# The first batch's attention laid out anew: x in runs of 1 KB, scores with tokens in partitions

## The chip, the core and the metric

The kernel runs on one core of a Trainium2 chip. The core has five engines with queues of their own: TensorE (PE, matmuls; PEld is its weight loads), VectorE (DVE), ScalarE (ACT), GpSimd (POOL) and SyncE (SP, which here issues most DMAs). The metric is the device time of one execution in microseconds; lower is better. All data in the compute part are fp32.

## The reference

`x` is (B, H, S, D) = (8, 8, 512, 64), `state` is (8, 8, 32, 64), `w_in` is 512 x 2048 and `w_out` 2048 x 512; the weights arrive as 64-bit floats.

```python
scores  = scale * np.matmul(x, state.transpose(0, 1, 3, 2))      # tokens by states
a       = softmax(scores);   xread = np.matmul(a, state)
scores2 = scale * np.matmul(state, x.transpose(0, 1, 3, 2))      # states by tokens
a2      = softmax(scores2);  sread = np.matmul(a2, x)
y = concat([xread, sread], axis=2)            # (B, H, 512 + 32, D)
y = y.transpose(0, 2, 1, 3).reshape(B * 544, 512)
h = y @ w_in
g = h * erf(softplus(h))
out = g @ w_out                               # (4352, 512)
```

## The kernel before

**Attention folded into the weights.** The kernel never forms `xread`. For each batch and each group of 512 hidden columns it multiplies the states with `w_in` (the "mixed" states, `mixed_part` and `mixed_pair`, tile `m`: 256 rows, one for each head and state) and then multiplies these with the transposed softmax weights `aT` (256 rows by 512 tokens). That product is `h` transposed, in four blocks of 128 hidden columns by 512 tokens. Softplus and erf run on ACT, the product with `h` on DVE, and the second projection accumulates in four PSUM banks `o0` to `o3`.

**Weights.** They come in 16 pieces of 1 MB in the order two of `w_in`, two of `w_out`, and so on (`pieces`, four groups). A piece goes from DRAM into one of three `raw` buffers (`weight`, DMA at L146), and is turned into fp32 by two ACT instructions (L152, L154) and three DVE instructions (L155, L156, L157). After the last of these, `fetch()` issues the DMA of the next piece. `weights_in(j)` gives 256 columns of `w_in` in 2 KB runs of the source; the fp32 copy has the form (partition, piece, k, 256 columns).

**Batch 0.** While the weights arrive, batch 0 alone is worked on, group by group, with products of 512 columns (`first0`, L828: four blocks a group, two matmuls each; `soft` L832; `erf` L835; `times` L839; `project` L626). Later batches (L559, L701) use seven products for eight and keep their operands in other forms. The change touches their part, from about 110 us on, only in the layout of `w_in`.

**The opening, `attention0`.** x of batch 0 comes in four DMAs of 128 tokens each, two from ACT's queue and two from SP's (L111); each run is 64 floats, 256 bytes. The states of batch 0 follow on SP (L114), then the weights. TensorE warms up on the identity (`warm(8)`), transposes x to `xT` (16 transposes, L312, in the order in which the quarters land), transposes the states (`states`, L190, copied by ACT at L191) and makes the scores with states in partitions (`scored`, L205: eight matmuls of 512 tokens on 64x32 tiles). Since the softmax over states needs a state axis within a partition, DVE turns the scores in 32x32 blocks (L225), takes the largest (L227), subtracts (L229); ACT takes the exponential (L230); DVE sums (L236), inverts (L240, L241), multiplies (L243) and turns the result back into `aT` (L329). ACT copies the scores to `sc` (L323) for the second softmax, which follows much later (`rest()`, L332 to L341). Between these stand, at three places, the conversion of the first weight pieces, half of the first mixed states (L455, copied at L457 and L458) and 32 + 5 matmuls on the identity (`after_scores`, `before_sums`, `amid_sums`).

**Order.** The order of instructions on TensorE, DVE, ACT and SP is that of the program text (`in_order`). Queues are worked strictly in turn, so an instruction that waits holds up all behind it on its engine. The states of batches 1 to 7 are loaded by `load_st()` (L120, eight DMAs, 256-byte runs), called at L902, and transposed at L936 in the third group.

Of the kernel before, what the change touches and what calls it, by code (L numbers as in the profile page):

```python
# [9 lines left out]
F32 = mybir.dt.float32  # L10
# [7 lines left out]
def kernel(  # L18
# [90 lines left out]
    x_t[0] = xin.tile([P, NC, H, D], F32, name="x")  # L109
    for c in range(NC):  # L110
        (nc.scalar, nc.sync)[c % 2].dma_start(  # L111
            out=x_t[0][:, c], in_=x[0, :, P * c:P * c + P].rearrange("h p d -> p h d"))
    for e in range(2):
        nc.sync.dma_start(out=st[:, 0, D * e:D * e + D],  # L114
                          in_=state[0].rearrange("(i e) n d -> e i n d", e=2)[e])

    def load_st():
# [6 lines left out]
    w_in = const.tile([P, NF // 4, NK, 2 * P], F32, name="w_in")  # L124
    away = ring[:, :, 2].rearrange("p u k i t -> p u (k i t)").rearrange(
        "p u (j k f) -> p u j k f", k=NK, f=2 * P)
    pieces_in = [w_in[:, j] for j in range(NF // 4)] + \
        [away[:, j // 2, j % 2] for j in range(NF // 4)]
    of_group = [w_in[:, 2 * g:2 * g + 2] for g in range(2)] + [away[:, u] for u in range(2)]
    kept_in = dram.tile([2, P, NF // 4, NK * 2 * P], F32, name="kept_in")  # L130
# [4 lines left out]
    def weight(dst, src, shape):  # L135

        if src.dtype == F32:
            fetched.append(nc.sync.dma_start(out=dst, in_=src))
            return [lambda: None] * 2, [lambda: None] * 3
        i = shape[1]
        raw = act.tile([P, 2 * shape[0] * i], U32, name="raw", bufs=3)
        fetched.append(nc.sync.dma_start(out=raw.rearrange("p (o i) -> p o i", i=2 * i),  # L146
                                         in_=src.bitcast(U32)))
        words = raw.rearrange("p (n w) -> p n w", w=2)
        lo, hi = words[:, :, 0], words[:, :, 1]
        dst = dst.rearrange("p o i -> p (o i)")  # L150
        d = dst.bitcast(U32)
        return [lambda: nc.scalar.activation(out=dst, in_=hi.bitcast(F32), func=ACTF.Copy,  # L152
                                             scale=2.0 ** -112),
                lambda: nc.scalar.activation(out=lo, in_=lo, func=ACTF.Copy, scale=2.0 ** -29)], \  # L154
            [lambda: nc.vector.tensor_scalar(d, d, 3, None, op0=ALU.logical_shift_left),  # L155
             lambda: nc.vector.tensor_tensor(d, d, lo, op=ALU.add),  # L156
             lambda: nc.vector.scalar_tensor_tensor(out=d, in0=hi, scalar=0x80000000, in1=d,  # L157
                                                    op0=ALU.bitwise_and, op1=ALU.bitwise_or)]
# [3 lines left out]
    def weights_in(j):  # L162
        return weight(pieces_in[j],
                      moe_w_in[:, 2 * P * j:2 * P * j + 2 * P].rearrange("(k p) f -> p k f", p=P),
                      (NK, 2 * P))

    def weights_out(j):
        return weight(w_out[:, 2 * j:2 * j + 2, :],
                      moe_w_out[2 * P * j:2 * P * j + 2 * P].rearrange("(t p) e -> p t e", p=P),
                      (2, d_model))  # L170

    spare = ps_o.tile([P, d_model], F32, name="o3")
# [9 lines left out]
    sT = const.tile([P, NK, B, Ns], F32, name="sT")  # L182
    aT = {}

    def states(bs, pool=ps_at, name="at"):


        ps = pool.tile([P, len(bs), P], F32, name=name)
        for k, b in enumerate(bs):
            last = nc.tensor.transpose(out=ps[:, k], in_=st[:, b, :], identity=ident)  # L190
        nc.scalar.copy(st[:, bs[0]:bs[-1] + 1, :], ps)  # L191
        return last

    over = lambda t: t.unsqueeze(2).to_broadcast([P, NC * NI, Ns])

# [23 lines left out]
    def states_weights(b, sc, both):  # L219

        aT[b] = keep.tile([P, 2, S], F32, name="aT")
        a = both[:, 0:2].rearrange("p e (k n) -> p e k n", n=Ns)
        m1 = small.tile([P, 2, NC * NI], F32, name="m1")
        for e in range(2):
            nc.vector.transpose(out=both[:, e], in_=sc[e])  # L225
        for e in range(2):
            nc.vector.reduce_max(out=m1[:, e], in_=a[:, e], axis=AX.X)  # L227
        for e in range(2):
            nc.vector.tensor_tensor(a[:, e], a[:, e], over(m1[:, e]), op=ALU.subtract)  # L229
            nc.scalar.activation(out=a[:, e], in_=a[:, e], func=ACTF.Exp, scale=scale)  # L230
        return a

    def sums(a):
        z1 = small.tile([P, 2, NC * NI], F32, name="z1")
        for e in range(2):
            nc.vector.reduce_sum(out=z1[:, e], in_=a[:, e], axis=AX.X)  # L236
        return z1

    def normalise(a, z1):
        nc.vector.tensor_scalar(z1, z1, 1e-9, None, op0=ALU.add)  # L240
        nc.vector.reciprocal(z1, z1)  # L241
        for e in range(2):
            nc.vector.tensor_tensor(a[:, e], a[:, e], over(z1[:, e]), op=ALU.mult)  # L243

# [14 lines left out]

    def inverse(z):  # L260
        nc.vector.tensor_scalar(z, z, 1e-9, None, op0=ALU.add)
        nc.vector.reciprocal(z, z)
# [37 lines left out]
    def attention0(between):  # L300

        xt = x_t[0]
        xT = att.tile([P, NI, S], F32, name="xT")
        xp = [ps_o.tile([P, S], F32, name="o%d" % i) for i in range(3)]
        xp.append(ps_h.tile([P, S], F32, name="h"))
        for c in 1, 0, 2, 3:
            if c == 2:
                warm(3)  # L310
            for i in range(NI):
                nc.tensor.transpose(out=xp[i][:, P * c:P * c + P],  # L312
                                    in_=xt[:, c, 2 * i:2 * i + 2, :], identity=ident)
        for i in range(NI):
            (nc.scalar.copy, nc.vector.tensor_copy)[i % 2](xT[:, i, :], xp[i])
        states(range(1), ps_h, "h")
        s2 = scored(0, xT)
        between[0]()
        both = att.tile([P, NI, S], F32, name="xT")
        sc = att.tile([P, 2, S], F32, name="sc")  # L320
        a = states_weights(0, s2, both)
        for e in range(2):
            nc.scalar.copy(sc[:, e], s2[e])  # L323
        between[1]()
        z1 = sums(a)
        between[2]()
        normalise(a, z1)
        for e in range(2):
            nc.vector.transpose(out=aT[0][:, e], in_=both[:, e])  # L329

        def rest():
            a2 = both[:, 2:4]  # L332
            m2 = largest(sc)
            yield
            z2 = weigh_tokens(sc, m2, a2)
            inverse(z2)
            yield
            a2T = turn_weights(a2)
            yield
            read_tokens(0, a2T, z2)  # L340
            yield  # L341

        return rest()

    def all_of(jobs):
        for f in jobs:
            f()
# [914 lines left out]
```

## Time and profile before

| | |
|---|---|
| median of 8 runs | 725.71 us (725.48 to 726.61) |
| the profiled execution | 725.54 us, its span 723.7 us |
| granted TensorE clock | 1.00 |
| first product with `aT` (L828) | at 22.00 us |
| TensorE busy from 0 to 22 us | 17.95 us, of which the identity matmuls of L177 are most |
| DVE busy from 10 to 20 us | 8.38 of 10 us |
| ACT busy from 25 to 40 us | 14.66 of 15 us |
| TensorE busy from 40 to 100 us | 59.88 of 60 us |

Times within the execution count from the start of the span. The profile lists, for each instruction, its start, its length and what ended the idle time before it; from this it builds a chain that leads from the last instruction back to the first. An engine's instructions overlap a little at their ends, so where an engine is busy without a break the distance between starts is shorter than one instruction's length. A matmul on fp32 appears as two entries, each with its weight load.

### The profile page before, as it was taken

Reading aid. Unit: us, or ns where it says so; the run is one execution under the profiler, and the core shown is the slowest. Engines: PE = TensorE matmul, PEld = TensorE weight load, DVE = VectorE, ACT = ScalarE, POOL = GpSimd, SP = SyncE. Lnnn points to the kernel's source line nnn. Section 1 sums busy time; section 2 is a strip of 40 time slices with the busy share of each in tenths; the row PEclk is TensorE's granted clock in tenths of the full one; section 3 lists DMA queues with packets and bytes.
Section 4 is the critical chain, followed back from the end, with each engine's and each line's share of the span. In section 5 each row is a group of like instructions: output and inputs, shape, how many; then the busy total and the mean of one; then the engine's idle time right before and its main releaser. Section 6 shows DMA issues by size and latency. Waiting matters only on the chain.

```text
span 723.7 us, 10832 instructions
## 1 busy us (share of the span) xinstructions
PE 713.7 (99%) x4232; PEld 564.3 (78%) x4232; DVE 537.3 (74%) x860; ACT 372.1 (51%) x536; POOL 25.2 (3%) x34
## 2 busy tenths in 40 slices
PE   8899999999999999999999999999999999999997
PEld 7444436588878878887888878887888888889996
DVE  4887779899868988788776967698777756665533
ACT  4899794636363624645346536463464534342340
POOL 0000000000100000000000000000000000000000
PEclk9999999999999999999999999999999999999999
DMA  7568886560239154422714270614232231102101
GB/s 236 180 206 250 227 223 240 140 191 29 41 78 232 21 125 61 109 77 70 125 20 154 59 135 13 175 27 133 45 82 103 72 67 19 39 30 30 20 12 29
DMA packets 142907, 74.64 MB, mean 103 GB/s; under 512 B 127112, under 2 KB 127368, under 8 KB 141320
## 3 DMA queue, kind: packets, MB, share of 16 engines
q1 hardware_dynamic: 136552, 65.89, 32.8%
q0 software_dynamic: 4032, 7.34, 7.5%
q10 hardware_dynamic: 2272, 0.72, 0.5%
q8 instruction: 33, 0.54, 0.4%
q14 instruction: 18, 0.15, 0.1%
HBM read 49.81 MB, written 20.45 MB: 97 GB/s over the span
## 4 chain that ended last, share of the span: by engine, by line
PE 93%; ACT 3%; DVE 2%; DMA 1%; issue 0%; ACTq 0%; DVEq 0%
PE o L701 47%; PE h L559 13%; PE at L559 10%; PE o L626 6%; PE h L604 3%; PE o L676 3%; PE h L828 2%; PE h L442 2%; PE at L442 1%; PE at L285 1%; PE at L828 1%; PE at L455 1%; DMA x<-in_x_dram 1%; PE h L205 1%; ACT L835 1%; PE at L205 0%
## 5 line engine op out<-in xcount | busy, mean ns | idle before, releaser
L701 PE MATMUL o<-w_out,ring 128*128 128x256 f32 x896 | 203.0, 379 | 0.0
L701 PEld LDWEIGHTS o<-w_out,ring 128*128 128x128 f32 x896 | 169.8, 190 | 25.0 <-DVE ring L1074 1.0
L701 PE MATMUL o<-raw,ring 128*128 128x256 f32 x672 | 161.4, 381 | 0.0
L701 PEld LDWEIGHTS o<-raw,ring 128*128 128x128 f32 x672 | 126.5, 190 | 25.9 <-ACT m L444 5.0
L552 ACT ACTIVATE ring<-ring 128x512 f32<-128x512 f32 x112 | 70.6, 631 | 59.9 <-DVE ring L542 59.3
L559 PE MATMUL h<-aT,m 128*128 128x256 f32 x336 | 82.0, 380 | 0.0
L1074 DVE TENSOR_TENSOR ring<-ring 128x1024 f32<-128x1024 f32 x60 | 70.6, 1219 | 3.9 <-ACT ring L616 3.9
L559 PEld LDWEIGHTS h<-aT,m 128*128 128x128 f32 x336 | 63.7, 190 | 10.4 <-DVE ring L542 0.7
L542 DVE TENSOR_TENSOR ring<-ring,at 128x512 f32<-128x512 f32 x84 | 57.1, 680 | 16.9 <-PE at L559 15.2
L626 PE MATMUL o<-w_out,ring 128*128 128x512 f32 x128 | 58.5, 597 | 1.4 <-DVE ring L839 1.4
L686 DVE TENSOR_TENSOR ot<-uv,o 128x256 f32<-128x256 f32 (+1 forms) x56 | 30.9, 553 | 30.4 <-PE o L701 28.4
L542 DVE TENSOR_TENSOR ring<-ring,h 128x512 f32<-128x512 f32 x56 | 38.0, 678 | 19.7 <-PE h L559 19.6
L724 ACT COPY ot<-o 128x256 f32<-128x256 f32 x28 | 10.4, 372 | 79.6 <-PE o L701 79.6
L761 POOL DMA_DIRECT2D out_dram<-ot x28 | 24.5, 943 | 659.4 <-DVE ot L686 609.6
L626 PEld LDWEIGHTS o<-w_out,ring 128*128 128x128 f32 x128 | 23.7, 190 | 29.4 <-issue 24.6
L686 DVE TENSOR_TENSOR ot<-ot,o 128x256 f32<-128x256 f32 x56 | 22.2, 416 | 27.8 <-ACT ot L724 27.7
L574 ACT COPY ring<-h 128x512 f32<-128x512 f32 x28 | 16.4, 586 | 47.9 <-PE h L559 47.9
L733 DVE TENSOR_TENSOR ring<-ring 128x512 f32<-128x512 f32 x56 | 38.6, 689 | 1.4
L734 DVE TENSOR_TENSOR ring<-ring 128x512 f32<-128x512 f32 x56 | 36.3, 685 | 0.0
L565 ACT COPY ring<-h 128x512 f32<-128x512 f32 x28 | 16.4, 586 | 28.3 <-PE h L559 28.3
L616 ACT ACTIVATE ring<-ring 128x2048 f32<-128x2048 f32 x16 | 30.4, 1902 | 0.0
L444 ACT COPY m<-h 128x512 f32<-128x512 f32 x11 | 6.4, 586 | 44.4 <-PE h L442 44.3
(181 smaller groups left out, 971.3 us busy)
## 6 DMA issues: line engine op xcount, KB each, us to landing
w_in<-kept_in SPq DMA_DIRECT2D x7, 2048.0 KB, 8.6
raw<-in_moe_w_in_dram SPq DMA_DIRECT2D x8, 1024.0 KB, 5.6
raw<-in_moe_w_out_dram SPq DMA_DIRECT2D x8, 1024.0 KB, 7.1
out_dram<-ot SPq DMA_DIRECT2D x32, 256.0 KB, 2.2
xq<-in_x_dram SPq DMA_DIRECT2D x112, 64.0 KB, 2.4
x<-in_x_dram SPq DMA_DIRECT2D x56, 128.0 KB, 3.1
out_dram<-ot POOLq DMA_DIRECT2D x28, 256.0 KB, 4.6
sc<-xT SPq DMA_DIRECT2D x112, 32.0 KB, 1.9
```

What stands on the lines that cost most here:

```text
L442: nc.tensor.matmul(out=ps[k][e][q, :], lhsT=st[r, b, q], rhs=of_group[g][r, :, i, :], start=True, stop=True)
L542: add = lambda o, x, y: nc.vector.tensor_tensor(o, x, y, op=ALU.add)
L552: nc.scalar.activation(out=s[k], in_=hs[k], func=ACTF.Softplus)
L559: nc.tensor.matmul(out=out[:, i], lhsT=x[:, q:q + P], rhs=y, start=(first and i == 0), stop=(i == 1), skip_group_check=not first)
L616: nc.scalar.activation(out=s, in_=s, func=ACTF.Erf)
L626: nc.tensor.matmul(out=acc[r], lhsT=gT[:, i, P * r:P * r + P], rhs=w_out[:, GF * g + i, :], start=(g == 0 and i == 0), stop=(g == NG - 1 a ...
L686: add = lambda o, x, y: tt(o, x, y, op=ALU.add)
L701: nc.tensor.matmul(out=out, lhsT=lhs[:, i, :], rhs=rhs[:, g, i, :], start=(start and i == 0), stop=(i == GF - 1), skip_group_check=not start)
L733: return [lambda: tt(S1, A21, A22, op=ALU.add), lambda: tt(S2, S1, A11, op=ALU.subtract), lambda: tt(S3, A11, A21, op=ALU.subtract), lambd ...
L734: lambda: tt(S3, A11, A21, op=ALU.subtract), lambda: tt(S4, A12, S2, op=ALU.subtract)]
L761: nc.gpsimd.dma_start(out=rows[2 * h + r][:, c], in_=ot[:, c], accum_op=ALU.add)
L1074: nc.vector.tensor_tensor(s[:, ks], s[:, ks], hs[:, ks], op=ALU.mult)
```

## The change

**x and the states.** x of batch 0 now comes in four DMAs by pairs of heads. Partition p gets tokens 4p to 4p+3, so each run is 4 x 64 floats, 1 KB. The rows of `out` for batch 0 are addressed in the same order (`put_x`). The states of batch 0 come twice side by side, (4 heads x 32 states) in partitions, two groups of heads, in two DMAs on SP between the second and the fourth of x.

**Scores.** For each head, a tile of two tokens-quarters by 64 channels is transposed to `xT` (128 x 128). A block-diagonal tile `bd` holds, for each head, its transposed states twice, so that one matmul of 128 rows gives the scores of two token quarters, with tokens in partitions (`score`: 16 matmuls of 64 columns). The states axis lies within a partition, and the softmax (`less`, `total`, `shared`) runs by two groups of four heads straight from PSUM; its weights are then transposed on TensorE (four transposes a group) and copied by ACT (`keep_a`). The scores with states in partitions, for the second softmax, are 32 matmuls of 128 columns on 64x32 tiles; they stay in the banks `o2` and `o3` until DVE copies them (`keep_scores`). 16 matmuls on the identity follow them, where 32 and 5 stood.

**Weights.** `w_in` is kept as (partition, block of 128 columns, k, 128 columns); each piece is fetched in two DMAs of 128 columns, with runs of 1 KB. The first piece is converted in two halves (two sets of two ACT and three DVE instructions), and the first mixed states of group 0 are made in quarters, quarter, half.

**States of the other batches.** `load_st()` is called before the opening, behind the first three pieces; their transposes go to the first group, in banks `o0` and `o1`, with ACT's copies behind the first erf.

**Other places.** The mixed states of batch 0 are placed by the table `where`, which gives each head its group and its 32 partitions. The identity matmuls write a bank of the pool `ps_h` in place of `o3`. `hidden_states`, `combine_s`, `bring` and `bring_last` follow the new layout of `w_in`.

```diff
-    x_t[0] = xin.tile([P, NC, H, D], F32, name="x")
-    for c in range(NC):
-        (nc.scalar, nc.sync)[c % 2].dma_start(
-            out=x_t[0][:, c], in_=x[0, :, P * c:P * c + P].rearrange("h p d -> p h d"))
-    for e in range(2):
-        nc.sync.dma_start(out=st[:, 0, D * e:D * e + D],
-                          in_=state[0].rearrange("(i e) n d -> e i n d", e=2)[e])
+    for i in range(NI):
+        (nc.scalar, nc.sync)[i % 2].dma_start(
+            out=x0[:, 2 * i:2 * i + 2].rearrange("p h c d -> p h (c d)"),
+            in_=x[0, 2 * i:2 * i + 2].rearrange("h (p c) d -> p h (c d)", c=NC))
+        if i == 1:
+            for k in range(2):
+                nc.sync.dma_start(out=st0[:, :, k],
+                                  in_=state[0].rearrange("(g h) n d -> (h n) g d", g=2))
...
+        blocks = [(raw, src)]
+        if len(src.shape) == 4:
+            blocks = [(raw.rearrange("p (h x) -> p h x", h=2)[:, h], src[:, h]) for h in range(2)]
+        for to, part in blocks:
+            part = part.bitcast(U32)
+            fetched.append(nc.sync.dma_start(
+                out=to.rearrange("p (a b) -> p a b", a=part.shape[1]), in_=part))
...
+        return weight(pieces_in[j], moe_w_in[:, 2 * P * j:2 * P * j + 2 * P].rearrange(
+            "(k p) (h f) -> p h k f", p=P, f=P), 2 if j == 0 else 1)
...
+        def score(g, hs):
+            if g not in tm:
+                tm[g] = ps_at.tile([P, NC, NI, Ns], F32, name="at")
+            for h in hs:
+                for k in range(2):
+                    nc.tensor.matmul(out=tm[g][:, 2 * k:2 * k + 2, where[h][1]],
+                                     lhsT=xT[:, h, k], rhs=bd[:, h], start=True, stop=True)
+
+        def less(g):
+            t = tm[g].rearrange("p c q n -> p (c q) n")
+            nc.vector.reduce_max(out=m1[:, g], in_=t, axis=AX.X)
+            tt(a[g], t, over(m1[:, g]), op=ALU.subtract)
+            nc.scalar.activation(out=a[g], in_=a[g], func=ACTF.Exp, scale=scale)
...
+        def shared(g):
+            tt(a[g], a[g], over(z1[:, g]), op=ALU.mult)
+            tp[g] = ps_o.tile([P, S], F32, name="o%d" % g)
+            for c in range(NC):
+                nc.tensor.transpose(out=tp[g][:, P * c:P * c + P],
+                                    in_=A[:, g, c].rearrange("p q n -> p (q n)"), identity=ident)
...
+        for i in 0, 1:
+            turn(i)
+            keep_x(i)
+        ps = ps_h.tile([P, 2 * P], F32, name="h")
+        for g in range(2):
+            nc.tensor.transpose(out=ps[:, P * g:P * g + P],
+                                in_=st0[:, g].rearrange("p k d -> p (k d)"), identity=ident)
+        for k in range(2):
+            r = slice(D * k, D * k + D)
+            nc.vector.tensor_copy(bd[r, :, k], ps[r].rearrange("p (h n) -> p h n", n=Ns))
+        for i in 2, 3:
+            turn(i)
+            keep_x(i)
+        nc.scalar.copy(st00, ps)
+        score(0, range(4))
+        score(1, range(4, 8))
+        s2 = [ps_o.tile([P, 2, 2, P], F32, name="o%d" % (2 + k)) for k in range(2)]
+        for h in range(H):
+            i, e = h // 2, h % 2
+            for c in range(NC):
+                r = slice(D * (c % 2), D * (c % 2) + D)
+                nc.tensor.matmul(out=s2[c % 2][Ns * i:Ns * i + Ns, e, c // 2],
+                                 lhsT=st00[r, Ns * h:Ns * h + Ns], rhs=xT[r, h, c // 2],
+                                 start=True, stop=True)
+        warm(16)
+        on_act("i", 0, [0])
+        less(0)
+        on_act("i", 0, [1])
+        less(1)
+        on_dve("i", 0, [0])
+        on_act("i", 0, [2, 3])
+        total(0)
+        on_act("i", 1)
+        on_dve("i", 0, [1])
+        shared(0)
+        total(1)
+        on_dve("i", 0, [2])
+        on_act("o", 0, [0])
+        keep_a(0, nc.scalar.copy)
+        m_t[0, 0] = mix.tile([P, 2, gw], F32, name="m")
+        mixed_part(0, 0, 0, 4, nc.scalar.copy, nc.scalar.copy)
+        shared(1)
+        on_act("o", 0, [1])
+        keep_a(1, nc.scalar.copy)
...
-    first0(0, 0, g0[0])
+    first0(0, 0, g0[0], [0])
+    on_dve("i", 0, [3, 4, 5])
+    mixed_part(0, 0, 1, 4, nc.scalar.copy, nc.scalar.copy)
+    first0(0, 0, g0[0], [1])
     first0(0, 1, g0[0])
     on_dve("i", 1)
     soft(0, g0)
-    on_act("o", 0, [1])
-    on_dve("o", 0, [0])
-    on_dve("o", 0, [1])
     soft(1, g0)
     mixed_part(0, 0, 1, 2, nc.scalar.copy, nc.scalar.copy)
-    on_dve("o", 0, [2])
+    keep_states = [states(range(1, 5), "o0")]
+    on_dve("o", 0)
     erf(A, g0)
     times(A, g0)
-    on_act("o", 1)
     for i in 2, 3:
         first0(0, i, g0[0])
+        if i == 2:
+            keep_states.append(states(range(5, B), "o1"))
+            all_of(keep_states)
+            keep_scores()
+            on_act("o", 1)
         soft(i, g0)
```

## The prediction

> **What bounds the kernel now.** First the page: busy shares and the chain that ended last, by engine.
>
> ```profile
> PE 713.7 (99%) x4232; PEld 564.3 (78%) x4232; DVE 537.3 (74%) x860; ACT 372.1 (51%) x536; POOL 25.2 (3%) x34
> ...
> PE 93%; ACT 3%; DVE 2%; DMA 1%; issue 0%; ACTq 0%; DVEq 0%
> ```
>
> TensorE owns the chain, though its busy time counts the matmuls on the identity (L177) that compute nothing. So time is to be had only where the chain is on another engine. The chain in order of time (start, length, what) shows where that is:
>
> ```profile
> 1.26 6.52 DMA x<-in_x_dram
> ...
> 8.75 1.30 DVE xT L315 x2
> ...
> 10.19 1.19 PE at L205 x16
> ...
> 11.46 1.31 DVE xT L225 x2
> ...
> 13.94 0.61 DVE xT L229
> ...
> 21.23 0.63 DVE aT L329
> ...
> 22.00 3.69 PE h L828 x8
> ...
> 38.52 1.24 DVE w_in L156
> 39.78 1.24 DVE w_in L157
> ...
> 41.06 0.67 PE at L455 x16
> ...
> 62.61 0.76 PE at L190 x7
> ...
> 86.43 1.03 PE at L285 x64
> ```
>
> Until 22.00 the chain is DMA and DVE; from there to 41.06 it is shared with ACT and DVE (erf, softplus, conversion of the third w_in piece); from 41.06 to 95 it is TensorE almost without a hole. The change works before 41.06, so its worth is how much earlier the matmul now at 41.06 can start, plus TensorE work taken out behind it. The timeline of the opening (start, length, engine, line; in brackets idle time before) gives the prices:
>
> ```profile
> 1.36 3.78 PE L177 MATMUL o<-ident 128*128 128x128 f32 x16 [1.36 <-POOL ident masks.py:199]
> ...
> 9.22 0.30 PE L190 MATMUL h<-ident,st 128*128 128x128 f32 x1 [0.29 <-DMA st<-in_state_dram]
> ...
> 10.19 1.09 PE L205 MATMUL at<-xT,st 64*32 64x512 f32 x16 [0.67 <-DVE xT L315]
> 11.21 7.41 PE L177 MATMUL o<-ident 128*128 128x128 f32 x64
> ```
>
> A pass of 128 columns takes 0.24 us at the start (3.78/16) and 0.116 later (7.41/64). An fp32 matmul is two passes. The granted clock stands at 1.00 all along, so it doesn't show this step; the transposes of x at 4.93 to 6.43 are still 0.215 apart, those from 7.83 on 0.113. Last, one-microsecond windows (PE, PEld, DVE, ACT, POOL busy; clock; DMA share; GB/s):
>
> ```profile
> 4.00:5.00 1.00, 1.00 (x7) 1.00 (x6) 0.00 (x0) 0.00 (x0) 0.00 (x0) 1.00 1.34 235
> ...
> 6.00:7.00 1.00, 1.00 (x9) 1.00 (x9) 0.00 (x0) 0.00 (x0) 0.00 (x0) 1.00 1.35 231
> ...
> 12.00:13.00 1.00, 1.00 (x12) 1.00 (x11) 1.00 (x3) 1.00 (x2) 0.00 (x0) 1.00 1.06 426
> ```
>
> The 256-byte runs of x fill the DMA engines at 231 GB/s; the 2 KB runs of w_in get 426.
>
> **x and the states.** x in 1 KB runs isn't shown; it lies between 231 and 426 GB/s. 1 MB then takes 2.5 to 4.5 us in place of 4.5, so its last quarter lands between 5.8 and 7.8. But the eight opening matmuls end at 5.14 either way, and 16 transposes plus two of the states follow in order: 0.215 each to 6.43, 0.113 after. That puts the first eight at 6.6, the states' two at 6.85, the last eight at 7.75. So x matters only past 7.3. DVE is the narrower: copy of the second pair (6.85, 0.61 as L315), then two copies of 64x256 for the block-diagonal tile (0.35 each, half of L315), so the score matmuls start at 8.3, against 10.19 for L205. That needs the states by 6.7. Before, they held L190 until 9.2; now they are issued at about 1.3 in place of 1.92 and lie ahead of the last quarter of x. I take 8.3 and keep 10.4 (states again at 9.2, then 0.2 transposes, 0.9 turning the last pairs) as the other end.
>
> **TensorE in the opening.** Scores with tokens in partitions: 16 matmuls of 64 columns on 128x128 weights, 32 passes. The trace has no such pass. L285 has 64 columns and 128x32 weights at 1.03/64 = 16 ns, four strips side by side, so 64 ns a strip; L177 has the weights but 128 columns, 116 ns. So 2.05 to 3.7; the two are equally near, and I take 2.9. The scores with states in partitions become 32 matmuls of 128 columns on 64x32 tiles, 64 passes of 0.107 (a 512-column pass of L626 is 0.43). L205 runs eight tiles at once: packed so, 0.9; one by one, 6.9. In the new order neighbours share one output strip and alternate between the two row halves, so two can run together: 3.4. Warm-up falls from 64 passes to 32: 3.7. In order, TensorE is free for the transposes of the softmax at F = 8.3 + 2.9 + 3.4 + 3.7 = 18.3.
>
> **DVE and ACT up to F.** Gone from DVE: four 32x32 transposes (2 x 1.31) and nothing else of size. The second subtraction (L229), which ended at 15.1, ends at T = 8.3 + 2.9 + 0.2 + 1.26 = 12.65. After it DVE has a half conversion, sum, reciprocal (0.4 + 0.95 + 0.65) and the product 0.64: T + 2.65 = 15.3, before F. ACT has one exp, the second half of piece 0, piece 1 and half of w_out (0.6 + 1.1 + 2.1 + 1.04): T + 4.85 = 17.5, before F + 0.65. So TensorE's queue decides.
>
> **From F to the matmul now at 41.06.** In order on ACT, with TensorE's replies between: four transposes and a latency 0.65; copy of aT 0.53; two 128-wide copies 0.45 (L191: 0.285, overlapping); conversion 1.05; second aT copy 0.55; two more small copies 0.45; table 1.28; softplus at 5.0; the second waits for TensorE (first products 3.3 to 5.85) and ends at 6.5; copies behind mixed states 7.1; table and erf 9.35; the states' copies, moved here from 63.30, 0.94: 10.3; w_out piece 2.1; table, two softplus, table, erf 4.55: 16.95; w_in piece 2.1: 19.05; DVE 1.24 + 1.24 and latency: F + 21.6. TensorE reaches its second projection half at 17.8 and is through at 21.2, so it isn't later than this. DVE's three conversions (T + 12.85 = 25.5) and the two score copies that it takes over from ACT lie in its holes. F + 21.6 = 39.9 against 41.06: **-1.2**.
>
> **Behind it.** Seven transposes (L190, 0.76) leave a stretch where TensorE is the chain: **-0.76**; they now lie in its wait at F + 6.5. Eight state loads leave the SP queue at 44.70, where they shared the DMA engines with a w_in piece that ACT then awaited for 0.63; off the chain, counted 0. They go behind the first w_out piece, in a hole of the DMA (102, then 0 GB/s at 15 to 19). w_in in 1 KB runs and twice the issues: at 231 GB/s a piece takes 4.5 us in place of 2.5; pieces are needed about every 4 us alternating with w_out, and they land mostly 4 us ahead: 0, up to +1. Other weight layout: same instruction sizes, 0.
>
> Placing a batch's mixed states by groups of four lets both row halves write one PSUM bank, where before each had its own; L455 shows 16 passes in 0.59 with two banks apart, and no row shows the other. The Trainium skill ("TensorEngine Tiling (Array Packing)", Gotcha 1) says that different row tiles cannot access the same bank at once. If that serialises them, six halves of 256 columns gain 0.43 each, an estimate by that page of +2.6 in all, and the sum becomes +0.6. I go by the row, since the two halves write different partitions.
>
> Sum: -1.2 - 0.76 = -1.9 on the profiled execution's 725.54 (span 723.7 plus 1.8 around it): 723.6. The median of the eight, 725.71, is 0.17 above it, which is noise here.
>
> **Rivals.** (1) Small passes cost less: 64 ns and fully packed, 2.05 + 0.9. Then F would be 14.95 and ACT rules instead (T 11.8, + 4.85 = 16.65, so an effective F of 16.0): 37.6, -3.5 - 0.76: 721.3. For: L205 and L285 pack well. Against: the order within a strip.
> (2) The opening isn't earlier: states land at 9.2 as now. Start 10.4, F 20.4, 42.0: +0.9 - 0.76, so 725.7. For: the 0.29 wait at L190. Against: earlier issue, fewer bytes ahead.
> (3) Slower: many small passes on TensorE take the place of DVE transposes, and nothing overlaps: 3.7 + 6.9. F = 22.6, 44.2, +3.1 - 0.76: 727.9. It decides once F passes 20.2 (41.06 + 0.76 - 21.6). For: 96 passes in a strict queue ahead of the softmax's transposes, where 16 stood. Against: L205.
> The Trainium skill ("TensorE: Matmul & The Clock Gate", Part 4) holds that transposes don't count as busy for the clock, which speaks for a late warm-up here; the trace has eight of them straight before the step at 6.43, in the same place as the new ones, so no run here separates the two. By that page the passes up to 9.8 would cost double, an estimate of some +1.5, and the sum would be about -0.4.
>
> **How the numbers follow.** Forecast 0.52 (own range 722.6 to 725.0, F from 17.3 to 19.7), rival 1 0.18, rival 2 0.12, rival 3 0.18. A measurement of this kernel tells about 0.2%, 1.45 us, from nothing. Faster by more: 0.18 + 0.42 of the forecast = 0.60; within: 0.09 of the forecast and nearly all of rival 2 = 0.20; slower: rival 3 and what the 1 KB runs may add, 0.20. The range takes in rival 1 and rival 2 and cuts rival 3: 720.9 to 726.9.
>
> **What would show it.** Score matmuls starting at 8.3 (right) or past 10 (rival 2); their 32 passes and the next 64 taking 2.9 and 3.4; the softmax's first transposes at 18.3, without a wait on DVE; the first 512-column product at about 19.8 in place of 22.00; the first mixed states of the second group at 39.9; no L190 in the sixties. The forecast is wrong if F comes from ACT or DVE, if a w_in piece lands late after 40, or if the mixed states' 16 passes grow beyond 0.67.

## The result and the profile after

The changed kernel takes 723.88 us (median of 12 runs, 723.28 to 724.30) beside 725.86 us for the kernel before (32 runs, 725.14 to 726.79): a ratio of 0.9971 with an interval of 0.9963 to 0.9978, or 2.0 us less. Forecast was 723.6. The profiled execution took 724.17 us, its span 722.3.

The page of the changed kernel, busy shares and the chain by engine:

```profile
PE 714.4 (99%) x4289; PEld 565.2 (78%) x4289; DVE 538.3 (75%) x866; ACT 372.8 (52%) x540; POOL 25.2 (3%) x34
...
PE 95%; ACT 3%; DVE 1%; issue 1%; POOL 0%; ACTq 0%; POOLq 0%
```

Before, DMA and DVE held 3% of the chain; now DMA is gone and DVE is at 1%. The chain in order of time (start, length, what) shows what stands in their place:

```profile
1.36 3.78 PE h L194 x16
5.14 1.71 PE o L311 x8
...
8.48 3.76 PE at L329 x32
12.23 2.41 PE o L375 x64
14.65 3.77 PE h L194 x32
18.41 0.45 PE o L346 x4
18.89 0.59 ACT aT L352
...
27.89 0.85 ACT st L211 x2
...
40.26 0.67 PE at L529 x16
...
59.08 0.59 PE at L529 x16
...
61.58 1.72 PE h L905 x4
...
111.58 2.67 PE h L633 x12
```

From 1.36 to 18.86 the chain is TensorE, but for DVE's copies from 6.88 to 8.34 (a pair of x, then the two into the block-diagonal tile). Then ACT, TensorE and DVE share it, and from 40.26 to 93 it is TensorE. Four rows of the two chains give the account:

| | before | after | difference |
|---|---|---|---|
| mixed states of group 1 start | 41.06 | 40.26 | -0.80 |
| length of the mixed states at 59.88 and 59.08 | 0.82 | 0.59 | -0.23 |
| from their end to the products (L828 at 63.37, L905 at 61.58) | 2.67 | 1.91 | -0.76 |
| first products of batch 1 start (L559, L633) | 113.36 | 111.58 | -1.78 in all |

The last row is the mark used below, since everything after it runs alike: the last DVE instruction starts at 718.12 in place of 719.91. Between these two profiled spans the difference is only 1.4, because what follows that instruction, the last store of `out`, took 4.2 in place of 3.8; the medians differ by 2.0.

The timeline of the opening (start, length, engine, line, operation; in brackets idle time before):

```profile
4.94 1.90 PE L311 MATMUL o<-ident,x 128*128 128x128 f32 x8
...
7.48 0.85 DVE L363 COPY ring<-h 64x256 f32<-64x256 f32 x2
...
8.48 3.76 PE L329 MATMUL at<-ring,xT 128*128 128x64 f32 x32 [0.22 <-DVE ring L363]
12.16 2.48 PE L375 MATMUL o<-xT,ring 64*32 64x128 f32 x64
...
18.25 0.60 PE L346 MATMUL o<-ident,ring 128*128 128x128 f32 x4
...
19.70 1.12 PE L905 MATMUL h<-aT,m 128*128 128x512 f32 x2
```

Here are the terms of the forecast: score matmuls at 8.48 behind DVE's copies, their 32 passes 3.76, the 64 passes with states in partitions 2.48, then 32 on the identity until 18.4, and the first product of 512 columns at 19.70 in place of 22.00. The 2.30 gained here is 0.80 at the mixed states of group 1. Of it 1.42 is left when the first products end (24.26 against 25.68), since they now pause for the second quarter of the mixed states and the second copy of `aT`; 1.63 at the first erf (26.84 against 28.47); and the two copies of states behind that erf (L211, 0.85), which are new there, take it down to 0.8.

The windows (busy of PE, PEld, DVE, ACT, POOL; clock; DMA share; GB/s) of the changed kernel:

```profile
4.00:5.00 1.00, 1.00 (x7) 1.00 (x6) 0.00 (x0) 0.00 (x0) 0.00 (x0) 1.00 1.14 352
...
10.00:11.00 1.00, 1.00 (x11) 1.00 (x10) 0.52 (x1) 0.00 (x0) 0.00 (x0) 1.00 1.09 374
```

The first row falls while x arrives in 1 KB runs: 352 GB/s, where 256-byte runs got 235 in the same window before. The next two windows have 263 and 333, where 217 and 231 stood. The second row falls while `w_in` arrives in 1 KB runs.

### The profile page after: what moved, and what is told of

It is laid out like the page before. It is cut to its first block, busy times and chain, and to the rows that moved or that the text cites. A ratio compares the mean times of both kernels' runs of the same rounds, so it can differ in the third digit from the quotient of the medians.

```text
span 722.3 us, 10976 instructions
## 1 busy us (share of the span) xinstructions
PE 714.4 (99%) x4289; PEld 565.2 (78%) x4289; DVE 538.3 (75%) x866; ACT 372.8 (52%) x540; POOL 25.2 (3%) x34
## 4 chain that ended last, share of the span: by engine, by line
PE 95%; ACT 3%; DVE 1%; issue 1%; POOL 0%; ACTq 0%; POOLq 0%
PE o L775 47%; PE h L633 13%; PE at L633 10%; PE o L700 6%; PE h L678 3%; PE o L750 3%; PE h L905 2%; PE h L512 2%; PE at L512 1%; PE at L282 1%; PE h L194 1%; PE at L905 1%; PE at L529 1%; PE h L232 1%; PE at L329 1%
## 5 line engine op out<-in xcount | busy, mean ns | idle before, releaser
L633 PE MATMUL h<-aT,m 128*128 128x256 f32 x336 | 82.0, 380 | 0.0
L633 PEld LDWEIGHTS h<-aT,m 128*128 128x128 f32 x336 | 63.7, 190 | 10.4 <-DVE ring L616 0.7
L700 PE MATMUL o<-w_out,ring 128*128 128x512 f32 x128 | 58.8, 598 | 1.5 <-DVE ring L916 1.5
L700 PEld LDWEIGHTS o<-w_out,ring 128*128 128x128 f32 x128 | 23.7, 190 | 29.9 <-issue 24.4
```

The source lines that it names most:

```text
L633: nc.tensor.matmul(out=out[:, i], lhsT=x[:, q:q + P], rhs=y, start=(first and i == 0), stop=(i == 1), skip_group_check=not first)
L700: nc.tensor.matmul(out=acc[r], lhsT=gT[:, i, P * r:P * r + P], rhs=w_out[:, GF * g + i, :], start=(g == 0 and i == 0), stop=(g == NG - 1 a ...
```

## The experiments

All start from the changed kernel unless said. Each time stands beside runs of the kernel before on the same chip, whose medians were 725.6 to 725.9; the ratio is against those.

**The states of the other batches back in their old place.** They are loaded again behind the start of group 1 and their transposes stand in the third group again.

```diff
-        ps = ps_o.tile([P, len(bs), P], F32, name=name)
+        ps = ps_at.tile([P, len(bs), P], F32, name=name)
...
-    load_st()
...
-    keep_states = [states(range(1, 5), "o0")]
...
-            keep_states.append(states(range(5, B), "o1"))
-            all_of(keep_states)
...
+    load_st()
...
+    for bs in range(1, 5), range(5, B):
+        states(bs, "at")()
```

> The changed kernel with one part undone: the states of batches 1 to 7 are loaded, transposed and copied at their old place in the third group. Theory: from the first softplus to the third w_in piece ACT has no free time, so the two copies of states cost the opening their 0.85 us there, and what the move gains later (0.77 us of transposes on TensorE, 0.23 us by a w_in piece that no longer shares the DMA with the states) is about the same. Then the mixed states now at 40.26 start at 39.4, the transposes stand in the sixties again, and the whole is 0.1 to 0.4 us slower than the changed kernel: 724.0 to 724.3. Rival, the prediction's own sum: the move is worth its 0.76 us in full and costs nothing early; then the mixed states stay at 40.2 and the time is 724.6 to 724.9.

It took 724.16 us, 0.9974 (0.9964 to 0.9984). The chain of this run:

```profile
39.20 0.67 PE at L529 x16
...
60.53 0.77 PE at L210 x7
...
111.28 2.67 PE h L633 x12
```

The mixed states start at 39.20, 1.06 earlier than with the move; 0.19 of that is an opening whose transposes happened to run faster (below), so ACT's early copies of the states cost about 0.87 (0.85 in the chain above). The seven transposes are back on the chain for 0.77. The two cancel within 0.3 at the last mark. So the -0.76 of the prediction is there, and its price, 0.87 of ACT ahead of 40, is there too: the move as a whole is worth nothing that can be measured. The mixed states at 58.02 last 0.59 here as well, though the loads are at their old place, so the 0.23 gained at 59 doesn't come from moving them.

What it comes from shows in the timelines, the first two lines before, the others after the change:

```profile
58.69 1.28 DVE L839 TENSOR_TENSOR ring<-ring,at 128x512 f32<-128x512 f32 x2 [1.98 <-ACT ring L835]
59.81 0.89 PE L455 MATMUL at<-ring,st 64*32 64x256 f32 x16
...
57.18 1.28 DVE L916 TENSOR_TENSOR ring<-ring,at 128x512 f32<-128x512 f32 x2 [1.23 <-ACT ring L912]
59.01 0.66 PE L529 MATMUL at<-ring 64*32 64x256 f32 x16
```

The mixed states write the two banks `at` that DVE's two products read. Before, the second product ended at 59.97: one pass started at 59.81 and no other until 60.0. After the change it ended at 58.46, and in this run at 57.35, and the passes start together. DVE was late before because it follows ACT's erf, and ACT had waited 0.63 for a `w_in` piece ahead of that erf (at 51.67). In the changed kernel and in this run ACT has no such wait ahead of the erf. Why that piece is in time here too, with the loads of states back beside it, is open.

**No matmuls on the identity behind the scores.**

```diff
-        warm(16)
```

> The changed kernel without the 16 matmuls on the identity before the softmax's transposes. Theory: ACT is as late as TensorE there (its half of the first w_out piece ends at 18.5, the copy of aT starts at 18.89), so TensorE is free 3.8 us earlier and only 0.4 us of it is seen: 723.5, first 512-column product at 19.3 in place of 19.70. Rival, the prediction's words that TensorE's queue decides: the transposes follow DVE's product at 16.3, and all behind them comes 1.5 to 2 us earlier: 722.0. A third: the idle time lets TensorE's passes fall back to 0.215 us for 128 columns, and the kernel gets slower than 724.5.

It took 723.79 us, 0.9975 (0.9966 to 0.9984). Its timeline:

```profile
16.29 0.66 PE L346 MATMUL o<-ident,ring 128*128 128x128 f32 x4 [1.68 <-DVE ring L343]
...
18.42 0.56 ACT L352 COPY aT<-o 128x512 f32<-128x512 f32 x1
19.18 1.12 PE L904 MATMUL h<-aT,m 128*128 128x512 f32 x2
```

In the profiled execution TensorE is free of 3.77 us of work and makes the transposes 2.0 earlier, but the copy that waits for them starts only 0.47 earlier (18.42 against 18.89), because ACT is in the half piece of `w_out` (L167) until then. The mark gains 0.31 (111.27). "TensorE's queue decides" is thus true by half a microsecond and no more. The next thing late is the conversion of the first weight piece on DVE (its last instruction ends at 20.35, and the second quarters of the mixed states start at 20.49).

The other executions show what the identity matmuls do besides. In six of the eleven the mean granted clock is 0.998 or more, and they took 723.22 to 723.79; in five it is 0.995 to 0.997, and they took 724.13 to 725.72. None of the 24 executions of the changed kernel, its repeat below among them, is under 0.998. So the third theory, that idle time slows TensorE, came true in a part of the executions, two of them above its 724.5; the experiment "The same without the identity matmuls" below shows it in a trace.

**Eight neighbours on eight tiles.** The 64 passes with states in partitions, in an order in which eight matmuls in a row stand on eight different tiles (four strips of output partitions, two row halves).

```diff
-        for h in range(H):
-            i, e = h // 2, h % 2
-            for c in range(NC):
+        for e, k in ((e, k) for e in range(2) for k in range(2)):
+            for h, c in ((2 * i + e, 2 * k + j) for i in range(NI) for j in range(2)):
+                i = h // 2
```

> The changed kernel with the 32 matmuls of the states-in-partitions scores put in an order in which eight neighbours use eight different tiles (both row halves, all four strips); before, eight in a row shared one strip. Theory: the 64 passes, 2.41 us now, are 2.6 times as fast as one by one and pack to 0.9 to 1.1 us; the softmax's transposes come at 17.1 in place of 18.41, but ACT isn't free for the copy of aT before 18.5, so no more than 0.4 us reaches the end: 723.5 to 723.9. Rival: the strips don't matter and each pass costs its own start (38 ns); then 2.4 us stays.

It took 723.93 us, 0.9975 (0.9966 to 0.9984). Its timeline of TensorE:

```profile
8.08 0.65 PE L311 MATMUL o<-ident,x 128*128 128x128 f32 x4 [1.09 <-DMA x<-in_x_dram]
...
12.18 1.16 PE L375 MATMUL o<-xT,ring 64*32 64x128 f32 x64
...
16.94 0.60 PE L346 MATMUL o<-ident,ring 128*128 128x128 f32 x4
```

The 64 passes fall from 2.48 to 1.16: order among tiles is worth 1.3 us of TensorE. As with the identity matmuls, little of that reaches the end (mark 111.22, -0.36; the median shows none of it). The first row was not foreseen by either theory: the last quarter of x came 1.09 late.

**x in 256-byte runs again**, tokens in the old order; all else as changed.

```diff
-            out=x0[:, 2 * i:2 * i + 2].rearrange("p h c d -> p h (c d)"),
-            in_=x[0, 2 * i:2 * i + 2].rearrange("h (p c) d -> p h (c d)", c=NC))
+            out=x0[:, 2 * i:2 * i + 2].rearrange("p h c d -> p (h c) d"),
+            in_=x[0, 2 * i:2 * i + 2].rearrange("h (c p) d -> p (h c) d", p=P))
...
-        rows = out[TB * b:TB * b + S].rearrange("(p c) e -> c p e" if b == 0 else
-                                                "(c p) e -> c p e", p=P)
+        rows = out[TB * b:TB * b + S].rearrange("(c p) e -> c p e", p=P)
```

> The changed kernel with x of batch 0 in 256-byte runs again, tokens in their old order; all else as changed. Theory: TensorE comes to the second half of x only at 6.9, and x in short runs lands at 7.2 to 7.8, so the score matmuls start at 8.5 to 9.0 in place of 8.48 and the end moves by 0 to 0.5 us: 723.9 to 724.4. Rival: the earlier landing of x is where the opening's gain comes from; then the scores start at 10 or later and the time is 725.2 to 725.7.

It took 724.69 us, 0.9986 (0.9977 to 0.9995), 0.8 more than the changed kernel; its mark is 112.18, 0.6 later. Its timeline of TensorE, then its windows from 5 to 7 us, with columns as above, and two pieces of its chain:

```profile
5.72 1.09 PE L311 MATMUL o<-ident,x 128*128 128x128 f32 x8 [0.57 <-DMA x<-in_x_dram]
7.62 0.41 PE L359 MATMUL h<-ident,ring 128*128 128x128 f32 x2 [0.80 <-DMA ring<-in_state_dram]
...
9.07 3.75 PE L329 MATMUL at<-ring,xT 128*128 128x64 f32 x32
```

```profile
5.00:6.00 1.00, 0.43 (x4) 0.28 (x4) 0.00 (x0) 0.00 (x0) 0.00 (x0) 1.00 1.34 217
6.00:7.00 1.00, 0.81 (x8) 0.57 (x6) 0.15 (x1) 0.59 (x1) 0.00 (x0) 1.00 1.35 218
```

```profile
2.38 6.16 DMA x<-in_x_dram
...
8.58 0.66 PE o L311 x4
```

At 217 GB/s the states, which follow half of x, land at 7.6, the last quarter of x at 8.54, and the scores start 0.59 later. The chain runs through that last quarter and its four transposes; DVE's copies of the states end at 8.92 and would have held the scores almost as long, so the two are level. So the 1 KB runs carry 0.6 to 0.8 of the 2.0, somewhat more than my theory gave them, and the rival that all of the gain is theirs falls.

**The states' copies on DVE** in place of ACT, the first of them ahead of the first erf.

```diff
-        return lambda: nc.scalar.copy(st[:, bs[0]:bs[-1] + 1, :], ps)
+        return lambda: nc.vector.tensor_copy(st[:, bs[0]:bs[-1] + 1, :], ps)
...
     on_dve("o", 0)
+    keep_states[0]()
...
-            all_of(keep_states)
+            keep_states[1]()
```

> The changed kernel with the two copies of the transposed states (0.85 us on ACT behind the first erf) made by DVE, which idles 1.1 us there and 2.0 us before the second products. Theory: ACT is the chain between the first erf and the third w_in piece, so the mixed states at 40.26 come 0.8 us earlier and stay so to the end: 723.1. Rival: TensorE's second projection half, which ended at 40.1, is next in line at once, or DVE's copies delay the first products: no gain, 723.7 to 724.2.

It took 723.04 us, 0.9962 (0.9949 to 0.9974). Its chain:

```profile
28.63 10.30 PE o L700 x24
38.93 0.59 PE at L529 x16
...
110.18 2.67 PE h L633 x12
```

The matmul that started at 40.26 starts at 38.93, and what stands ahead of it in the chain is no longer ACT and DVE but the second projection (L700): TensorE itself, back to back. Some 0.7 of the 1.33 is a faster start of this execution (its score matmuls begin at 7.78), so the copies are worth about 0.63 here (the medians differ by 0.84, with intervals that overlap). That is most of the price of the move that the first experiment had found, paid on an engine with holes.

**The same without the identity matmuls.**

```diff
-        warm(16)
```

> The changed kernel with the copies of states on DVE and without the 16 identity matmuls. Theory: with ACT relieved, TensorE has no hole from its first product to the projection's end, so the 0.46 us by which the products started earlier without the identity matmuls now counts, less what DVE's third w_in piece (ready 0.2 us before TensorE wants it) takes back: 0.2 to 0.4 us under the kernel with DVE's copies alone, 722.6 to 722.9. Rival: DVE's chain of conversions rules, no gain: 723.0.

It took 723.18 us, 0.9961 (0.9946 to 0.9977): no better than with them, and the expectation was missed. Its timeline and its windows show why; the last line is the same window of the earlier run without identity matmuls:

```profile
16.34 0.66 PE L346 MATMUL o<-ident,ring 128*128 128x128 f32 x4 [1.68 <-DVE ring L343]
18.06 0.68 PE L528 MATMUL at<-w_in,ring 64*32 64x128 f32 x16 [1.07 <-DVE w_in L174]
18.67 1.11 PE L346 MATMUL o<-ident,ring 128*128 128x128 f32 x4
19.58 1.79 PE L904 MATMUL h<-aT,m 128*128 128x512 f32 x2
```

```profile
18.00:19.00 1.00, 0.94 (x18) 0.59 (x19) 0.88 (x3) 1.00 (x3) 0.00 (x0) 0.50 0.05 8
20.00:21.00 1.00, 1.00 (x2) 0.00 (x0) 0.99 (x2) 0.84 (x2) 0.00 (x0) 0.50 0.00 0
...
18.00:19.00 1.00, 0.93 (x20) 0.62 (x20) 0.88 (x3) 1.00 (x3) 0.00 (x0) 1.00 0.00 0
```

Four transposes take 1.11 where the first four took 0.66, and two entries of 512 columns 1.79 where the changed kernel's took 1.12. Behind idle stretches of 1.68 and 1.07, with four transposes between, the granted clock fell to 0.50, from 17.7 to 21.1; the six entries from 21.68 on are at full pace again. In the profiled execution of the earlier run the same idle stretches brought no fall (clock 1.00), so it comes in some executions only. The six executions here say the same: three with a mean clock of 0.999 took 722.28, 722.80 and 722.98, about what was expected; three with 0.997 or 0.998 took 723.39 to 723.86. So the identity matmuls pay for their place by holding the clock, not by anything they compute.

**The first weight piece whole**, not in halves.

```diff
-            "(k p) (h f) -> p h k f", p=P, f=P), 2 if j == 0 else 1)
+            "(k p) (h f) -> p h k f", p=P, f=P))
...
-        on_act("i", 0, [2, 3])
...
-        mixed_part(0, 0, 0, 4, nc.scalar.copy, nc.scalar.copy)
+        mixed_part(0, 0, 0, 2, nc.scalar.copy, nc.scalar.copy)
...
-    on_dve("i", 0, [3, 4, 5])
-    mixed_part(0, 0, 1, 4, nc.scalar.copy, nc.scalar.copy)
```

> The changed kernel with the first w_in piece converted whole, and the first mixed states of group 0 made in two halves in place of quarter, quarter, half. Theory: DVE reaches the first mixed states 1.5 us later (0.27 + 0.6 + 0.6), at 19.4; but all four products then run without a break and end at about 24.3, as now (24.26), so the end moves by less than 0.4 us: 723.6 to 724.3. Rival: the halves are what lets the products start at 19.70; without them the end is 1 to 1.5 us later: 725.0 to 725.4.

It took 724.99 us, 0.9984 (0.9975 to 0.9994), 1.1 more than the changed kernel. My theory fell and the rival held. Its timeline:

```profile
20.65 1.18 ACT L169 ACTIVATE raw<-raw 128x1024 uint32<-128x1024 uint32 x1
21.71 0.60 ACT L352 COPY aT<-o 128x512 f32<-128x512 f32 x1
22.36 2.84 PE L904 MATMUL h<-aT,m 128*128 128x512 f32 x6 [0.68 <-ACT aT L352]
```

The mixed states of group 0 wait for the whole conversion, the first product starts at 20.55, 0.85 later, and on ACT the copies of the mixed states, the conversion (L169) and the second copy of `aT` follow in the same order as in the changed kernel but 0.95 later (that copy at 21.71 against 20.76); the mark is 112.57, 1.0 later. The halves, which the prediction had costed only within its chain and never by themselves, carry about half of the gain. Without them the first product still starts 1.45 ahead of the kernel before (22.00).

**The copies on DVE and the packed order together.**

> The changed kernel with the copies of states on DVE and the packed order of the small score matmuls, the 16 identity matmuls kept, so that TensorE has no idle stretch over 1 us before the softmax's transposes. Theory: the transposes come at about 17, the products run at full pace (1.1 us for the first two passes, where 1.8 was seen without the identity matmuls), and the 0.4 us that ACT's relief lets through is kept: 0.2 to 0.5 us under DVE's copies alone, 722.5 to 722.8. Rival: DVE's and ACT's conversions of the third w_in piece are next in line, and it stays at 723.0.

It took 723.26 us, 0.9965 (0.9953 to 0.9977), no better than the copies alone. The transposes come at 16.97, but the mixed states behind them wait 0.54 for DVE's conversion (L174, from 17.33), and x was late again, by 0.91. Time taken from TensorE before 18.4 goes into the wait for ACT and DVE: they are level.

**The changed kernel once more**, on another chip.

> The changed kernel itself once more, beside the one before on the same chip, as the yardstick for the packed one: 723.6 to 724.2 and a ratio of 0.9971 within 0.001 either way. In its profile the first eight transposes of x take either 1.9 or 1.2 us, as the pass length steps down after or before them; that alone moves the end by 0.7 us.

It took 724.19 us (11 runs, 723.97 to 725.24), 0.9981 (0.9972 to 0.9989): 1.5 us less than the kernel before on that chip, where the first runs gave 2.0. The first eight transposes of x took 1.66, neither of the two lengths expected. The profiled execution was its slowest, 725.24, and its timeline shows what made it so:

```profile
9.18 0.66 PE L311 MATMUL o<-ident,x 128*128 128x128 f32 x4 [1.87 <-DMA x<-in_x_dram]
9.67 3.68 PE L329 MATMUL at<-ring,xT 128*128 128x64 f32 x32
```

The last quarter of x lands at 9.1, 1.87 after TensorE was ready, the scores start 1.2 later and the mark is 112.73. Of nine profiles with this order of DMAs and 1 KB runs, three show TensorE idle for a late last quarter (1.87, 1.09, 0.91); in three more, the changed kernel's first profile among them, only a weight load waits for it, by some 0.3, and nothing behind is later for that. The size that a delay of the opening can have, which the prediction had put on the states, is real; its bearer is x.

**The last quarter of x from ACT's queue**, with the copies on DVE.

```diff
-        (nc.scalar, nc.sync)[i % 2].dma_start(
+        (nc.scalar, nc.sync, nc.scalar, nc.scalar)[i].dma_start(
```

> The kernel with the copies of states on DVE, and the last quarter of x issued from ACT's queue (behind the third) in place of SP's, where two DMAs of states lie ahead of it and w_in behind. Theory: in three of nine profiles of the 1 KB kernels so far TensorE waited 0.9 to 1.9 us for that last quarter and 0.5 to 1.2 us of it reached the score matmuls; issued 0.5 us earlier and on a queue without other traffic it lands before 6.9 each time, the wait is gone, and the median falls by 0 to 0.4 us below DVE's copies alone: 722.6 to 723.1. Rival: the last quarter is late because the DMA engines are shared, whichever queue issues it; the wait of 0.9 us or more stays in some profile and the time is 723.0 to 723.5.

It took 722.83 us (5 runs, 722.51 to 723.52), 0.9956 (0.9942 to 0.9970). Its timeline of TensorE:

```profile
7.12 0.41 PE L359 MATMUL h<-ident,ring 128*128 128x128 f32 x2 [0.39 <-DMA ring<-in_state_dram]
7.37 1.04 PE L311 MATMUL o<-ident,x 128*128 128x128 f32 x8
8.58 3.75 PE L329 MATMUL at<-ring,xT 128*128 128x64 f32 x32 [0.17 <-DVE ring L363]
```

All eight transposes run without a wait for x. The states are 0.39 late in their place. This is the fastest version of the study: 0.44% below the kernel before. Against the changed kernel it stands by 722.83 to 723.88, or to 724.19 in the repeat; the intervals of the two ratios still overlap at their ends (0.9970 and 0.9963). Beside the copies alone (723.04) the difference of 0.2 shows nothing. One profile without a late x, where three of nine had one, is no proof that the queue cured it.

**The last quarter of x ahead of the states on SP**, with the copies on DVE.

```diff
-        if i == 1:
+        if i == 3:
```

> The kernel with the copies of states on DVE, and SP issuing the last quarter of x before the two DMAs of states. Theory: x lands before 6.9, but the states land 0.3 to 0.7 us later, past the 6.6 at which TensorE asks for them, and the block-diagonal tile with them: scores start at 8.5 to 9.0, the time is 723.0 to 723.6. Rival: the states have slack too, and with x never late it gains as much as the queue of ACT: 722.6 to 723.1.

It took 723.81 us (7 runs, 723.73 to 724.14), 0.9972 (0.9960 to 0.9983): x is in time, but the states are 0.52 late, the scores start at 8.82, and 0.8 is lost against the copies alone (the intervals of these two overlap) and 1.0 against the run before this one on the same chip (no execution of the one is as short as any of the other: 723.73 or more against 723.52 or less). More than I had expected, and the rival fell too. In both of these profiles it is the states that are late, where with x last on SP it was x in three of nine.

## Why the prediction was right, by its own steps

- **Start of the scores, 8.3:** 8.48. Neither x nor the states held it. The first eight transposes ended at 6.85 in place of 6.6, but the working let DVE's copy start only at 6.85 (6.88); the 0.18 come from the two small copies (L363), 0.41 and 0.44 in the chain where 0.35 each was taken. Held here; the repeat shows 9.67. "x matters only past 7.3" stands, but "its last quarter lands between 5.8 and 7.8" is too narrow: up to 9.1.
- **32 score passes, 2.9 (2.05 to 3.7):** 3.76. Mis-sized by 0.86. A pass of 64 columns with 128x128 weights costs 3.76/32 = 0.1175, as much as one of 128 columns (L194, 3.77/32 = 0.118). The 32 weight loads beside them are busy for 3.65 us in both cases, so they, not the columns, set the price here, and the upper row was the right neighbour.
- **64 passes with states in partitions, 3.4 (0.9 to 6.9):** 2.41. Mis-sized by 1.0 the other way: neighbours on one strip took the time of nearly three at once, not two (64 x 0.107 / 2.41 = 2.8).
- **Identity matmuls, 3.7:** 3.77.
- **F = 18.3:** 18.41, by cancelling errors.
- **"So TensorE's queue decides":** half right. ACT's queue, for which T + 4.85 = 17.5 was worked out, was through at about 18.5, since T came at 13.7 in place of 12.65 with the longer score passes. Run by run, 1.3 to 3.8 us taken off TensorE brought 0.3 to 0.4 at the mark.
- **F + 21.6 = 39.9, -1.2:** 40.26, or F + 21.85; -0.80. The list of ACT's work behind F was right to 0.25 over 22 us, and the 0.25 is mostly a slip in adding: table, two softplus, table and erf stand in it with 4.55, where the rows of before give 4.75 (31.65 to 36.40), and 4.75 is what they took (30.85 to 35.60). Its row "the states' copies, 0.94" is the 0.87 that the first experiment gave back.
- **-0.76 for the transposes:** 0.76 as a row, about 0 as a move, since those copies are part of the -1.2 sum. The prediction had both terms and added them rightly, but did not see that the move nets nothing.
- **The wait of 0.63 for a w_in piece, counted 0 as off the chain:** 0.23 of it was on it, by way of ACT's erf, DVE's product and the bank that the mixed states write (first experiment). The wait is gone and with it the 0.23. With the loads put back ACT waits 0.59 for a w_out piece, but behind the erf (at 58.70), and the 0.23 stays gained: so moving the loads isn't what removed it.
- **w_in in 1 KB runs, 0 to +1:** 0; ACT waits for no piece after 40. The bytes came at 374 GB/s, where the estimate for the bad end took 231.
- **Two row halves in one bank:** the row decided rightly. The 16 passes take 0.67 and 0.59 (L529), as L455's did. The Trainium skill ("TensorEngine Tiling (Array Packing)", Gotcha 1) would have added an estimated 2.6 us; the runs show none of it where the halves write different partitions.
- **The clock:** the 32 score passes took 3.76 us at an even pace (9 entries in the first microsecond, 11 in each of the next two windows, which also count entries begun before). The working's estimate of doubled passes up to 9.8, from the Trainium skill ("TensorE: Matmul & The Clock Gate", Part 4: transposes don't count as busy in the same way), did not come true here.

In sum -0.80, -0.23 and -0.76 stand against -1.2, 0 and -0.76: 1.8 in the profiles, 2.0 in the medians (1.5 in the repeat), 1.9 forecast. That the sum came out so close is luck in part: errors of +0.86 and -1.0 in F cancel. Rival 1 (721.3) fails on its 64 ns: a score pass took 0.1175, so T came at 13.7 and ACT was through only at 18.5, where rival 1 had 16.65; the packed order alone, tried above, brought 0.36 at the mark. Rival 3 fails because its 3.7 for the scores came without its 6.9; rival 2's delay occurs in part (1.2 of 2.1) in some executions, by another load.

The one place where the working was blind: it took the gain as one queue's (TensorE's) and didn't ask what each part was worth alone. Measured so, the halves of the first piece carry 1.0 to 1.1, the 1 KB runs 0.6 to 0.8, the early states nothing. These are single removals, so they need not add to the whole. No run undoes the new scores (tokens in partitions) alone, so what they carry by themselves isn't shown; if the parts did add, 0.1 to 0.4 us would be left for them and all else.

## What to carry to other kernels

When a stretch has two queues within a microsecond of each other, shortening one brings only their distance; look at which instruction of the second would be late next before paying for the first. A move that takes work off the bounding engine in a later stage must be netted against what it puts on the bounding engine of the earlier one, and a copy is best put on the engine with holes there. Here a pass of 64 columns cost as much as one of 128 with the same weights, so price a matmul with few columns by the row with the same weights and not by that with the same columns. Before taking out matmuls that compute nothing, read the granted clock in the windows and over all executions: one profiled execution can miss the fall.

## What was not expected of the hardware

- **Order among tiles.** 64 passes of 64x32 weights by 128 columns took 2.48 us with eight neighbours on one strip of output partitions and 1.16 us with eight neighbours on eight tiles.
- **The pace of TensorE at the start changes at a point that isn't fixed.** The first eight transposes of x took 1.90 us in the changed kernel and 1.66 in its repeat, 1.17 and 1.21 in two variants with the same instructions up to there, and so moved everything behind by up to 0.7 us, with a granted clock of 1.00 in the windows throughout.
- **Short idle stretches can halve the granted clock.** Without the identity matmuls TensorE idled 1.68 and 1.07 us with 0.66 us of transposes between. In one profile the clock then read 0.50 for 3.4 us (17.7 to 21.1) and four transposes took 1.11 in place of 0.66; in another it stayed at 1.00. Over all executions of the first run without them, five of eleven have a mean clock of 0.997 or less; of 24 with them, none.
- **Loads of one queue.** The last 256 KB of x, behind two small loads on SP, kept TensorE idle in three of nine profiles, by 0.9 to 1.9 us; with the order turned, in one profile, the small loads were 0.5 late.
